# A gated mix of linear attention and experts: two subtractions of the weight preparation stand behind the last sum of a group's seventh slot instead of in front of it

## The chip, the cores and the metric

The kernel runs on one core of a Trainium2 chip. The metric is the time of one execution in device microseconds (us), from runs on the chip. Beside the runs there is one execution that was recorded by the hardware profiler; its trace is what the sections on the profile read.

TensorE (PE) multiplies matrices, with its weight loads shown apart (PEld). VectorE (DVE) and ScalarE (ACT) work element by element and read PE's results out of PSUM. GpSimd (POOL) and SyncE (SP) issue DMA transfers here.

## The reference

Tokens `x` (2048 x 512) go through two branches that a gate mixes. Cut to what matters:

```python
g = sigmoid((x * gate_w).sum(-1))            # the gate, one number for a token
pq, pk = phi(q), phi(k)                      # linear attention, 32 heads of 16
a = (pq @ (pk^T v) / (pq . sum(pk))) @ wo
for e in range(8):                           # all 8 experts, weighted by a softmax
    out += w[e] * (silu(x @ w1[e]) @ w2[e])  # w1[e] 512 x 1792, w2[e] 1792 x 512
return g * a + (1 - g) * out
```

Nearly all of the arithmetic is that of the experts' two layers.

## The kernel before

**Three products for one.** Operands are split into a high part (ScalarE copies the number, rounded to the matmul's type) and a low part (VectorE subtracts the high part from the number). A product is then three matmuls: high by high, high by low, low by high (`mm3`, lines 57 to 60). So every weight and every activation needs one ScalarE copy and one VectorE subtraction, each over 128 x 512 elements as a rule, before TensorE can use it.

**Seven products for eight.** Both layers use a Strassen-like scheme: of two by two blocks seven products are made. That takes sums and differences of blocks on VectorE.

**Groups, slots and ticks.** The first layer runs through 116 groups (an expert, two of its 14 column blocks, one half of the tokens). A group has seven slots, and the loop counter `u` is seven times the group `g` plus the slot `k`. In each slot TensorE does one product of the first layer, six matmuls of 512 columns. In slot 6, the seventh, it does product 5 into the bank `a`, and VectorE then adds that bank to the tile `s3` (line 692). TensorE goes on with product 0 of the next group in the other buffer of `a`, and in slot 1 it adds product 6 of the old group into the old bank `a`: for that the sum of line 692 must have read the bank. From `u` = 45 on there is also a tick of the second layer in every other slot, and from `u` = 72 on in every slot, again six matmuls (`p<-ho,w` in the rows). The activations `ho` that a tick reads are split three ticks or more ahead (line 768).

**The weights one group ahead.** While group `g` runs, `prep(g + 1, step)` splits the raw weights of the next group, a step in a slot. A group's `o` tiles hold the weights of the first layer: `o_0` is ready for product 0, `o_2` serves products 5 and 1, `o_3` products 3 and 4, `o_1` product 6. For the experts' first half of tokens the same steps also make the second layer's weights (`ws`, in the first groups `w` and `wx`) and SP writes them to DRAM (`w2stash`), from where they are loaded again for the ticks (line 793). The `ws` tiles have two buffers that go around.

**Order.** Nothing is scheduled by a tool: each engine runs its instructions in the order in which the program issues them. In a slot `other()` comes first (the step of `prep`, low parts of `ho`, differences between blocks, high parts of `ho`), then the product, then `mid()` with the tick, and last what reads the product's bank.

Of the kernel before, what the change touches and what calls it, by code (L numbers as in the profile page):

```python
# [37 lines left out]
def f32(ap):  # L38
    return ap.bitcast(F32)
# [100 lines left out]
def weights(m):  # L140
    nc, v, w1p, act_copy = m.nc, m.v, m.w1p, m.act_copy

    m.ORDER = ("P1", "P7", "P2", "P4", "P6", "P5", "P3")
    m.SEQ = {n: [(prod, q) for prod in m.ORDER for q in range(n)] for n in (2, NPAIR)}
    last = m.SEQ[NPAIR].pop(NPAIR - 1)
    m.SEQ[NPAIR].insert(2 * NPAIR - 2, last)
    raw, ops, ws = {}, {}, {}
    m.ops = ops
    m.spare = None


    def raw_tile(name, dt=F32):
        return w1p.tile([P, 2048], dt, name=name, tag="rm", bufs=2)


    def with_second(part):
        return part.e < E and part.h == 0

    def load(g):
        if g >= m.NG:  # L160
            return
        part, q = m.groups[g]
        both = with_second(part)
        if g >= m.G1 + 2:
            r = w1p.tile([P, 2 * D], F32, name=f"rs{g}", tag="ws", bufs=2)
            r = raw[g] = r.rearrange("p (r h w f) -> p r h w f", r=2, h=2, w=1)
        else:
            r = raw[g] = raw_tile(f"rm{g}").rearrange("p (r h w f) -> p r h w f", r=2, h=2, w=2)
        for i in range(2):
            if part.e < E:  # L170
                src = m.wm[part.e * NPAIR + q][:, i]
                nc.sync.dma_start(r[:, i, :, 0, :], src[:, :D].rearrange("p (h f) -> p h f", h=2))
            else:
                src = m.wq.rearrange("p (h k c f) -> p h k c f", h=2, k=2, c=KT)
                for h in range(2):
                    nc.sync.dma_start(r[:, i, h, 0, :].rearrange("p (k f) -> p k f", k=2), src[:, h, :, 2 * q + i, :])
        if both:
            for i in range(2):
                src = m.wm[part.e * NPAIR + q][:, i, D:]
                nc.sync.dma_start(r[:, :, i, 1, :], src.rearrange("p (h f) -> p h f", h=2))  # L180

    def two(o, c):
        return o[:, c].rearrange("p (h f) -> p h f", f=HALF)

    def o_tile(name, tag, bufs, width):
        return w1p.tile([P, 2, width], F32R, name=name, tag=tag, bufs=bufs)

    def stash(part, q, prod, src):
        i = part.e * 7 * NPAIR + m.SEQ[part.n].index((prod, q))
        nc.sync.dma_start(m.w2stash[i // 2][:, i % 2].rearrange("p (c f) -> p c f", c=2), f32(src))  # L190

    def prep(g, step):
        if g >= m.NG:
            return
        part, q = m.groups[g]
        r = raw[g]
        both = with_second(part)

        def high(n, src, *places):
            o = o_tile(f"o{g}_{n}", "o", 4, D)
            act_copy(two(o, 0), src)
            for i, at in places:
                ops[g][i] = o, at

        def low(i, src):
            o = ops[g][i][0]
            v.tensor_sub(two(o, 1), src, f32(two(o, 0)))  # L209


        def ws_tile(n):
            w = ws[g, n] = m.spare(f"wx{g}_{n}") if m.spare and n < 3 else o_tile(f"ws{g}_{n}", "ws", 2, D)
            return w

        def high2(n, src):
            if both:
                act_copy(two(ws_tile(n), 0), src)

        def low2(n, src, *prods):  # L220
            if both:
                w = ws.pop((g, n))
                v.tensor_sub(two(w, 1), src, f32(two(w, 0)))  # L223
                for half, prod in enumerate(prods):
                    stash(part, q, prod, w[:, :, half * HALF:(half + 1) * HALF])


        begin = part is m.parts[0] and q < 6

        def first(c):  # L230
            return m.first_w2(q)[:, c] if begin else ws[g, 0][:, c, :HALF]

        def block(i, j):
            return r[:, i, j] if both else r[:, i, j, 0]

        if step == 0:
            ops[g] = [None] * 7
            high(0, r[:, 0, :, 0], (0, 0), (2, HALF))
        elif step == 1:
            low(0, r[:, 0, :, 0])  # L240
            o = o_tile(f"o{g}_1", "oh", 2, HALF)
            act_copy(o[:, 0], r[:, 1, 1, 0])
            ops[g][6] = o, 0
            if both and not begin:
                ws_tile(0)
            if both:
                act_copy(first(0), r[:, 0, 0, 1])
            high2(1, r[:, :, 1, 1] if both else None)
        elif step == 2:
            o = ops[g][6][0]  # L250
            v.tensor_sub(o[:, 1], r[:, 1, 1, 0], f32(o[:, 0]))
            if both:
                v.tensor_sub(first(1), r[:, 0, 0, 1], f32(first(0)))
                stash(part, q, "P1", m.first_w2(q) if begin else ws.pop((g, 0))[:, :, :HALF])
        elif step == 3:
            low2(1, r[:, :, 1, 1] if both else None, "P2", "P4")
            v.tensor_add(block(1, 1), block(1, 0), block(1, 1))
        elif step == 4:
            v.tensor_sub(block(1, 0), block(0, 0), block(1, 0))
            v.tensor_sub(block(0, 0), block(1, 1), block(0, 0))  # L260
        elif step == 5:
            high(2, r[:, 1, :, 0], (5, 0), (1, HALF))
            high2(2, r[:, :, 0, 1] if both else None)
            v.tensor_sub(block(0, 1), block(0, 1), block(0, 0))
        elif step == 6:
            low(5, r[:, 1, :, 0])
            low2(2, r[:, :, 0, 1] if both else None, "P6", "P7")
            high(3, r[:, 0, :, 0], (3, 0), (4, HALF))
            high2(3, r[:, :, 1, 1] if both else None)
        else:  # L270
            low(3, r[:, 0, :, 0])
            low2(3, r[:, :, 1, 1] if both else None, "P3", "P5")


    wp = {}

    def load_wp(q):
        wp[q] = raw_tile(f"wr{q}")[:, :2 * D].rearrange("p (r h f) -> p r h f", r=2, h=2)
        for i in range(2):
            nc.sync.dma_start(wp[q][:, :, i], m.wpd[2 * q + i].rearrange("p (r f) -> p r f", r=2))  # L280

    def prep_wp(q, step):
        r = wp[q]

        def high(n, src):
            act_copy(two(wp["w"][n % 2], 0), src)

        def low(n, src, *prods):
            w = wp["w"][n % 2]
            v.tensor_sub(two(w, 1), src, f32(two(w, 0)))  # L290
            for half, prod in enumerate(prods):
                stash(m.A[0], q, prod, w[:, :, half * HALF:(half + 1) * HALF])

        if step == 0:
            both = raw_tile(f"ww{q}", F32R).rearrange("p (n c f) -> p n c f", n=2, c=2)
            wp["w"] = [both[:, n] for n in range(2)]
            act_copy(wp["w"][0][:, 0, :HALF], r[:, 0, 0])
            high(1, r[:, :, 1])
        elif step == 1:
            w = wp["w"][0]  # L300
            v.tensor_sub(w[:, 1, :HALF], r[:, 0, 0], f32(w[:, 0, :HALF]))
            stash(m.A[0], q, "P1", w[:, :, :HALF])
        elif step == 2:
            low(1, r[:, :, 1], "P2", "P4")
        elif step == 3:
            v.tensor_add(r[:, 1, 1], r[:, 1, 0], r[:, 1, 1])
            v.tensor_sub(r[:, 1, 0], r[:, 0, 0], r[:, 1, 0])
        elif step == 4:
            v.tensor_sub(r[:, 0, 0], r[:, 1, 1], r[:, 0, 0])
            v.tensor_sub(r[:, 0, 1], r[:, 0, 1], r[:, 0, 0])  # L310
        elif step == 5:
            high(2, r[:, :, 0])
            high(3, r[:, :, 1])
        elif step == 6:
            low(2, r[:, :, 0], "P6", "P7")
        else:
            low(3, r[:, :, 1], "P3", "P5")

    m.raw_tile, m.load, m.prep, m.load_wp, m.prep_wp = raw_tile, load, prep, load_wp, prep_wp

def keys(m):
# [208 lines left out]
    beside = {t: [] for t in range(NTT, NT)}  # L532
    for k in range(KT):
# [4 lines left out]
        beside[(10, 10, 12, 12)[k]].append(lambda k=k: x_sum(1, k))  # L538
        beside[(11, 11, 13, 13)[k]].append(lambda k=k: x_part(1, (1, 5, 3, 6)[k]))
        beside[14].append(lambda k=k: m.prep(0, k))  # L540
        beside[15].append(lambda k=k: m.prep(0, 4 + k))
    rows_of = {12: (12, 13), 13: (14, 15), 14: (), 15: ()}
    for t in range(NTT, NT):
        if t in (4, 8):
# [27 lines left out]
def experts(m, misc):  # L572
# [541 lines left out]
    for u in range(LAG + NTICK):  # L1114
# [3 lines left out]
        g, k = divmod(u, 7)  # L1118
# [43 lines left out]
        if u < NU + 3:  # L1162
            up(g, k, mid, other)
        else:
            other()
            mid()
        if u == 5:
            state()
        if u == 6:
# [79 lines left out]
```

## Time and profile before

| | |
|---|---|
| median of 3 runs | 2334.76 us (2334.21 to 2335.16) |
| the profiled execution, its own time | 2334.37 us |
| its span, first to last instruction | 2332.7 us |
| TensorE busy | 2324.6 us, 100% of the span |
| weight loads (PEld) | 1926.1 us, 83% |
| VectorE busy | 1802.6 us, 77% |
| ScalarE busy | 1404.4 us, 60% |
| GpSimd busy | 162.3 us, 7% |

The profiled execution's own time is 1.7 us more than its span, for what lies before the first and behind the last instruction. Busy shares are means over stages that differ: VectorE is over 80% busy up to some 1100 us, while second-layer weights are prepared, and about 72% later. TensorE's matmuls overlap, each is shown with some 390 ns while one starts about every 226 ns; so a busy share of 100% tells that it hardly idles, and the time lost shows in the distance from one matmul's start to the next.

### The profile page before, as it was taken

The page shows a single profiled execution, that of the slowest core. Times are in us where ns is not written, and L with a number is a line of the kernel's source. Part 1 is how long each engine was busy: PE and PEld are TensorE (multiplying, and loading weights), DVE is VectorE, ACT ScalarE, POOL GpSimd, SP SyncE. Part 2 cuts the span into 40 slices and gives each one's busy share as a digit, 9 for nine tenths or more (in the row PEclk, how much of TensorE's full clock was granted, in tenths as well). Part 3 has the DMA queues.
Part 4 walks back from the last instruction along what each step waited for, and adds up shares of the span by engine and source line. Part 5 has one row for each costly group of instructions (what it writes and reads, how often), then busy time and mean ns, then how long its engine had stood idle before and what let it go on. Part 6 is the DMA issues. An engine that isn't in the chain of part 4 may idle for free.

```text
span 2332.7 us, 31250 instructions
## 1 busy us (share of the span) xinstructions
PE 2324.6 (100%) x10444; PEld 1926.1 (83%) x10444; DVE 1802.6 (77%) x3100; ACT 1404.4 (60%) x2631; POOL 162.3 (7%) x223
## 2 busy tenths in 40 slices
PE   9999999999999999999999999999999999999999
PEld 8878888888888888888888888888888888888887
DVE  6798878888888878888666777777677677776676
ACT  6687666666666657666555555555565555555553
POOL 1101000000000000000000000000011010000011
PEclk9999999999999999999999999999999999999999
DMA  7898888988888898888846566566557756565576
GB/s 228 232 306 260 279 276 257 280 261 266 267 268 276 257 286 259 265 267 270 292 145 191 164 208 180 159 190 184 158 166 191 219 163 200 172 190 171 151 241 206
DMA packets 313425, 524.92 MB, mean 225 GB/s; under 512 B 26976, under 2 KB 205296, under 8 KB 312880
## 3 DMA queue, kind: packets, MB, share of 16 engines
q1 hardware_dynamic: 286848, 471.85, 61.6%
q0 software_dynamic: 25568, 50.43, 11.4%
q8 instruction: 82, 1.34, 0.2%
q14 instruction: 79, 0.65, 0.1%
q10 hardware_dynamic: 848, 0.66, 0.1%
HBM read 351.04 MB, written 167.59 MB: 222 GB/s over the span
## 4 chain that ended last, share of the span: by engine, by line
PE 97%; DVE 1%; DMA 1%; ACT 0%; issue 0%; SPq 0%; POOL 0%; DVEq 0%; POOLq 0%
PE p L58 16%; PE p L60 16%; PE p L59 16%; PE a L58 9%; PE a L60 9%; PE a L59 9%; PE c L60 4%; PE c L58 4%; PE c L59 4%; PE b L60 2%; PE b L58 2%; PE b L59 2%; PE g L445 2%; PE y L58 1%; PE y L60 1%; PE y L59 1%
## 5 line engine op out<-in xcount | busy, mean ns | idle before, releaser
L58 PE MATMUL p<-ho,w 128*128 128x512 f32 x1620 | 631.4, 390 | 0.9 <-DVE d L859 0.6
L60 PE MATMUL p<-ho,w 128*128 128x512 f32 x1620 | 630.4, 389 | 0.0
L59 PE MATMUL p<-ho,w 128*128 128x512 f32 x1620 | 630.3, 389 | 0.0
L768 DVE TENSOR_TENSOR ho<-s,ho 128x512 fp32r<-128x512 f32 x784 | 537.0, 686 | 71.0 <-ACT ho L63 67.3
L63 ACT ACTIVATE ho<-s 128x512 fp32r<-128x512 f32 x784 | 487.1, 623 | 22.0 <-PE p L60 10.4
L58 PEld LDWEIGHTS p<-ho,w 128*128 128x128 f32 x1620 | 304.1, 188 | 66.8 <-ACT p L63 2.3
L60 PEld LDWEIGHTS p<-ho,w 128*128 128x128 f32 x1620 | 304.0, 188 | 63.3
L59 PEld LDWEIGHTS p<-ho,w 128*128 128x128 f32 x1620 | 304.2, 188 | 62.8
L686 DVE TENSOR_TENSOR s<-c,s 128x512 f32<-128x512 f32 x116 | 80.2, 691 | 205.2 <-PE c L60 190.2
L63 ACT ACTIVATE o<-rs 128x512 fp32r<-128x512 f32 x224 | 129.2, 577 | 175.9 <-PE a L60 117.6
L63 ACT ACTIVATE o<-rm 128x512 fp32r<-128x512 f32 x240 | 137.5, 573 | 99.5 <-PE a L60 77.7
L63 ACT ACTIVATE ws<-rm 128x512 fp32r<-128x512 f32 x203 | 114.8, 573 | 76.7 <-DMA w2stash<-ws 69.6
L63 ACT ACTIVATE s<-a 128x512 f32<-128x512 f32 x116 | 69.4, 598 | 146.9 <-PE a L60 146.9
L615 ACT ACTIVATE s<-s 128x512 f32<-128x512 f32 x224 | 138.8, 620 | 14.5 <-DVE s L692 10.8
L615 ACT ACTIVATE s<-b 128x512 f32<-128x512 f32 x112 | 67.1, 599 | 107.0 <-PE b L60 106.9
L209 DVE TENSOR_TENSOR o<-rm,o 128x512 fp32r<-128x512 f32 x180 | 123.0, 683 | 0.7 <-ACT o L63 0.6
L209 DVE TENSOR_TENSOR o<-rs,o 128x512 fp32r<-128x512 f32 x168 | 114.7, 683 | 0.6 <-ACT o L63 0.6
L692 DVE TENSOR_TENSOR s<-a,s 128x512 f32<-128x512 f32 x116 | 79.9, 689 | 36.5 <-PE a L60 36.5
L223 DVE TENSOR_TENSOR ws<-rm,ws 128x512 fp32r<-128x512 f32 x154 | 105.5, 685 | 2.2 <-ACT ws L63 2.2
L63 ACT ACTIVATE b<-a 128x512 f32<-128x512 f32 x116 | 67.2, 579 | 56.8 <-PE a L60 56.7
L830 POOL DMA_DIRECT2D acct<-c x30 | 26.1, 871 | 880.7 <-DVE c L824 866.5
L63 ACT ACTIVATE s<-c 128x512 f32<-128x512 f32 x116 | 69.0, 595 | 27.2 <-PE c L60 27.1
(304 smaller groups left out, 4491.3 us busy)
## 6 DMA issues: line engine op xcount, KB each, us to landing
w<-w2stash SPq DMA_DIRECT2D x403, 512.0 KB, 4.1
w2stash<-ws SPq DMA_DIRECT2D x357, 256.0 KB, 4.4
rm<-wm SPq DMA_DIRECT2D x228, 256.0 KB, 5.1
rs<-wm SPq DMA_DIRECT2D x108, 256.0 KB, 4.1
wb<-wgtd SPq DMA_DIRECT2D x16, 512.0 KB, 5.8
acct<-c POOLq DMA_DIRECT2D x30, 256.0 KB, 6.1
acct<-d POOLq DMA_DIRECT2D x30, 256.0 KB, 5.8
acct<-k POOLq DMA_DIRECT2D x30, 256.0 KB, 5.8
```

The lines of the kernel that those rows point to most:

```text
L58: nc.tensor.matmul(ps, wh, xh, start=start, stop=False, skip_group_check=True)
L59: nc.tensor.matmul(ps, wh, xl, start=False, stop=False, skip_group_check=True)
L60: nc.tensor.matmul(ps, wlo, xh, start=False, stop=stop, skip_group_check=True)
L63: nc.scalar.activation(dst, src, AF.Copy, scale=scale, bias=bias)
L209: v.tensor_sub(two(o, 1), src, f32(two(o, 0)))
L223: v.tensor_sub(two(w, 1), src, f32(two(w, 0)))
L445: nc.tensor.matmul(ps, xk((0, 0, 1)[j], tb, k, tt * P, (tt + 1) * P), gw[g][:, (0, 1, 0)[j], k, :], start=(k == 0 and j == 0), stop=(k == ...
L615: nc.scalar.activation(dst, src, AF.Silu)
L686: v.tensor_add(sn[g, 2], bank[g, "c"], sn[g, 2])
L692: v.tensor_add(sn[g, 3], bank[g, "a"], sn[g, 3])
L768: v.tensor_sub(h[1], s, f32(h[0]))
L830: nc.gpsimd.dma_start(m.acct[part.h, j, dt], s, accum_op=ALU.add)
```

## The change

Step 6 of `prep` made the low part of `o_2` and, where there are second-layer weights, that of `ws_2`, and then two high parts. The two low parts are now a step of their own, 8, which is called in slot 6 after the product, the tick and the sum of line 692. The two high parts stay in step 6. Ahead of the main loop, where steps 4 to 7 of group 0 are called one after the other, the order is now 4, 5, 6, 8, 7.

```diff
-        elif step == 6:
+        elif step == 8:
             low(5, r[:, 1, :, 0])
             low2(2, r[:, :, 0, 1] if both else None, "P6", "P7")
+        elif step == 6:
             high(3, r[:, 0, :, 0], (3, 0), (4, HALF))
             high2(3, r[:, :, 1, 1] if both else None)
...
-        beside[15].append(lambda k=k: m.prep(0, 4 + k))
+        beside[15].append(lambda k=k: m.prep(0, (4, 5, 6, 8)[k]))
+    beside[15].append(lambda: m.prep(0, 7))
...
         else:
             other()
             mid()
+        if k == 6:
+            prep(g + 1, 8)
         if u == 5:
             state()
```

What this does to the order: TensorE, ScalarE, GpSimd and SP have the same instructions in the same order as before. VectorE has the same instructions, and from group 0's slot 6 on two of them (one where there are no second-layer weights) move down in each group. Two places of VectorE's order follow. Line numbers of the changed kernel are two higher from the main loop's functions on.

The first place is group 0's slot 6, where a one-off step of the attention branch, `kvt` (line 906, 908 after), comes behind the slot. `s_0<-c` is the sum of slot 5, `s_0<-a` that of slot 6. Before:

```order
L264 TENSOR_TENSOR rm_1206<-rm_1206 128x256
L686 TENSOR_TENSOR s_0_1426<-c_1395,s_0_1426 128x512
L209 TENSOR_TENSOR o_2_1428<-rm_1206,o_2_1428 128x512
L692 TENSOR_TENSOR s_0_1402<-a_1379,s_0_1402 128x512
L906 TENSOR_TENSOR kvt<-kv,mask 128x512
L209 TENSOR_TENSOR o_3_1456<-rm_1206,o_3_1456 128x512
```

And after:

```order
L264 TENSOR_TENSOR rm_1206<-rm_1206 128x256
L688 TENSOR_TENSOR s_0_1426<-c_1395,s_0_1426 128x512
L694 TENSOR_TENSOR s_0_1402<-a_1379,s_0_1402 128x512
L209 TENSOR_TENSOR o_2_1428<-rm_1206,o_2_1428 128x512
L908 TENSOR_TENSOR kvt<-kv,mask 128x512
L209 TENSOR_TENSOR o_3_1455<-rm_1206,o_3_1455 128x512
```

The low part of `o_2` has gone from ahead of the sum to between the sum and `kvt`; group 1 has no second-layer weights, so it is one instruction.

The second place is group 5's slot 6, the first with a low part of `ho` (line 768, 770 after) in it. Before:

```order
L686 TENSOR_TENSOR s_5_1987<-c_1956,s_5_1987 128x512
L209 TENSOR_TENSOR o_2_1989<-rm_1820,o_2_1989 128x512
L223 TENSOR_TENSOR wx_2_1991<-rm_1820,wx_2_1991 128x512
L768 TENSOR_TENSOR ho_1979<-s_2_1677,ho_1979 128x512
L692 TENSOR_TENSOR s_5_1963<-a_1926,s_5_1963 128x512
L209 TENSOR_TENSOR o_3_2005<-rm_1820,o_3_2005 128x512
L223 TENSOR_TENSOR ws_3_2007<-rm_1820,ws_3_2007 128x512
```

And after:

```order
L688 TENSOR_TENSOR s_5_1987<-c_1956,s_5_1987 128x512
L770 TENSOR_TENSOR ho_1979<-s_2_1677,ho_1979 128x512
L694 TENSOR_TENSOR s_5_1963<-a_1926,s_5_1963 128x512
L209 TENSOR_TENSOR o_2_1989<-rm_1820,o_2_1989 128x512
L223 TENSOR_TENSOR wx_2_1991<-rm_1820,wx_2_1991 128x512
L209 TENSOR_TENSOR o_3_2001<-rm_1820,o_3_2001 128x512
L223 TENSOR_TENSOR ws_3_2003<-rm_1820,ws_3_2003 128x512
```

The two low parts have moved down by two places; the low part of `ho` and the sum each stand two places further up. In later groups a difference between blocks can stand beside the `ho`, and it moves up with it.

## Rows read from the trace of the kernel before

**Rows 1.** The page's span, and the busy time of each engine, its share of the span and its instructions.

```profile
span 2332.7 us, 31250 instructions
PE 2324.6 (100%) x10444; PEld 1926.1 (83%) x10444; DVE 1802.6 (77%) x3100; ACT 1404.4 (60%) x2631; POOL 162.3 (7%) x223
```

**Rows 2.** Busy time by stretch of 100 us: the stretch and its length, then busy us and instructions of PE, PEld, DVE, ACT and POOL, the granted clock of TensorE as a share of full speed, the DMA share and GB/s.

```profile
100.00:200.00 100.00, 98.72 (x441) 78.92 (x440) 81.81 (x139) 75.36 (x146) 4.53 (x9) 1.00 0.90 288
...
400.00:500.00 100.00, 100.00 (x443) 82.81 (x442) 84.43 (x141) 63.33 (x119) 5.14 (x6) 1.00 0.88 272
```

**Rows 3.** Who waited for whom over the whole span: the engine, the tile and line that waited, what ended it, us in total, times, the longest.

```profile
DVE s L692 <- PE a L60: 36.5, 79, 3.6
...
PEld a L58 <- DVE s L692: 4.0, 6, 1.1
```

**Rows 4.** The timeline of TensorE at the six places that the last row counts: start, length, line, tiles. In each pair the first row is the last matmul of product 0 (`a<-x00h`), the second row the second matmul of product 6 (`a<-t6l`); one matmul (`a<-t6h`, L58) starts between them.

```profile
123.94 0.39 PE L60 MATMUL a<-x00h,o 128*128 128x512 f32 x1
...
124.61 0.40 PE L59 MATMUL a<-t6l,o 128*128 128x512 f32 x1
...
134.06 0.39 PE L60 MATMUL a<-x00h,o 128*128 128x512 f32 x1
...
135.48 0.39 PE L59 MATMUL a<-t6l,o 128*128 128x512 f32 x1
...
144.57 0.39 PE L60 MATMUL a<-x00h,o 128*128 128x512 f32 x1
...
145.24 0.40 PE L59 MATMUL a<-t6l,o 128*128 128x512 f32 x1
...
154.37 0.39 PE L60 MATMUL a<-x00h,o 128*128 128x512 f32 x1
...
155.03 0.40 PE L59 MATMUL a<-t6l,o 128*128 128x512 f32 x1
...
164.16 0.39 PE L60 MATMUL a<-x00h,o 128*128 128x512 f32 x1
...
165.43 0.40 PE L59 MATMUL a<-t6l,o 128*128 128x512 f32 x1
...
221.00 0.39 PE L60 MATMUL a<-x00h,o 128*128 128x512 f32 x1
...
222.16 0.39 PE L59 MATMUL a<-t6l,o 128*128 128x512 f32 x1
```

**Rows 5.** The timeline of VectorE in slots 5 and 6 of group 3, with idle time and what ended it in brackets, and last the end of product 5 on TensorE.

```profile
142.35 0.69 DVE L686 TENSOR_TENSOR s<-c,s 128x512 f32<-128x512 f32 x1 [0.63 <-PE c L60]
142.96 0.68 DVE L209 TENSOR_TENSOR o<-rm,o 128x512 fp32r<-128x512 f32 x1
143.56 0.69 DVE L223 TENSOR_TENSOR wx<-rm,wx 128x512 fp32r<-128x512 f32 x1
144.16 0.68 DVE L692 TENSOR_TENSOR s<-a,s 128x512 f32<-128x512 f32 x1
...
143.21 0.39 PE L60 MATMUL a<-t5h,o 128*128 128x512 f32 x1
```

**Rows 6.** The timeline at group 0's slot 6, VectorE, the weight load and TensorE: `wp<-wo,kvt` is a matmul that reads `kvt`.

```profile
108.76 0.69 DVE L692 TENSOR_TENSOR s<-a,s 128x512 f32<-128x512 f32 x1 [3.59 <-PE a L60]
...
109.37 0.68 DVE L906 TENSOR_TENSOR kvt<-kv,mask 128x512 f32<-128x512 f32 x1
...
110.10 0.30 PEld L910 LDWEIGHTS wp<-wo,kvt 128*128 128x128 f32 x2 [0.45 <-DVE kvt L906]
```

**Rows 7.** The timeline in group 2, around the step from slot 5 to slot 6: ScalarE copies bank `a`, which slot 4 left (`s<-a`), and TensorE goes from product 4 (`c<-x11h`) to product 5 into that bank (`a<-t5h`, then `a<-t5l`).

```profile
130.78 0.59 ACT L63 ACTIVATE s<-a 128x512 f32<-128x512 f32 x1
...
131.01 0.39 PE L60 MATMUL c<-x11h,o 128*128 128x512 f32 x1
...
131.76 0.39 PE L59 MATMUL a<-t5l,o 128*128 128x512 f32 x1
```

**Rows 8.** The timeline in group 9, slots 5 and 6, and group 10, slots 1 to 3: VectorE's two sums, ScalarE's copy of weights that waits for a DMA to DRAM, its copy into the second layer's bank (`p<-p`), and TensorE around the tick that uses this bank.

```profile
217.42 0.69 DVE L686 TENSOR_TENSOR s<-c,s 128x512 f32<-128x512 f32 x1 [0.25 <-PE c L60]
...
221.08 0.68 DVE L692 TENSOR_TENSOR s<-a,s 128x512 f32<-128x512 f32 x1
...
226.64 0.63 ACT L63 ACTIVATE ws<-rm 128x512 fp32r<-128x512 f32 x1 [1.47 <-DMA w2stash<-ws]
...
228.31 0.58 ACT L63 ACTIVATE p<-p 128x512 f32<-128x512 f32 x1
...
228.54 0.39 PE L60 MATMUL b<-x01h,o 128*128 128x512 f32 x1
...
229.28 0.39 PE L59 MATMUL p<-ho,w 128*128 128x512 f32 x1
```

**Rows 9.** A later stretch: VectorE's read of a second-layer bank in slot 0 of a group; then a load of second-layer weights that SP issues behind the writes of a slot 0, how long a load takes from issue to landing there, and the first matmul of the tick that reads it.

```profile
717.53 0.69 DVE L824 TENSOR_TENSOR e<-p,wb 128x512 f32<-128x512 f32 x1 [1.59 <-PE p L60]
...
358.05 0.41 SPq L793 DMA_DIRECT2D w<-w2stash  x1
...
DMA to landing us min/median/max: 6.9/6.9/6.9
...
367.81 0.39 PE L58 MATMUL p<-ho,w 128*128 128x512 f32 x1
```

## The prediction

> **What bounds the kernel now.** I read the page first: TensorE is busy for 2324.6 of 2332.7 us [rows 1], so only what lets TensorE start a matmul sooner or later can move the end. The view by stretches tells where it loses anything: from 300 to 2200 us every 100 us hold 443 matmuls (one such stretch is shown), which is one each 100/443 = 0.226 us and is the pace of an unbroken row; between 100 and 200 us there are 441, with TensorE busy for 98.72 us [rows 2]. The clock is granted in full in both. So in the long middle there is nothing to win, only to lose.
>
> The waits then tell what the sum of line 692 has to do with it. In 79 of 116 groups VectorE sits idle in front of it, waiting for TensorE, 36.5 us in total; in 6 groups it is the other way round and TensorE's weight load waits for the sum [rows 3]. TensorE's timeline shows these six places, all before 230 us [rows 4]. From the last matmul of product 0 to the second matmul of product 6 an unbroken row takes 2 x 0.226 = 0.45 us. It took 0.67, 1.42, 0.67, 0.66, 1.27 and 1.16 us, so the losses are 0.22, 0.97, 0.22, 0.21, 0.82 and 0.71: 3.15 us together. That is the most that an earlier sum can give.
>
> **The change, first part: the sum comes sooner.** Where VectorE arrives late, two subtractions in front of the sum go away. Their starts and the sum's lie 0.60 us apart (142.96, 143.56, 144.16 [rows 5]), so the sum can start up to 1.20 us sooner, but not before product 5 has ended. In group 3 that is at 143.21 + 0.39 = 143.60, so the sum starts at some 143.65 in place of 144.16 and ends near 144.35, while product 6 could start at 144.57 + 0.23 = 144.80. The wait of 0.22 goes. Groups 1 and 4 have the same pattern and size. Group 2 lost 0.97 and has 1.20 to gain; group 5 lost 0.82. In group 5 a low part of `ho` stays in front of the sum, but its high part was made a slot earlier, so it holds nothing up. In group 9 `ho` and a difference stay in front: from 217.42 three places of 0.60 put the sum at 219.2 in place of 221.08 [rows 8]. All six waits should go.
>
> **Second part: what takes some of it back.** Two places downstream are held by ScalarE, not by VectorE.
> In group 2 product 5 waits for ScalarE's copy that ends at 130.78 + 0.59 = 131.37; the row from 131.01 to 131.76 is 0.30 longer than 0.45 [rows 7]. ScalarE works without a pause from 120 us to there and nothing in it depends on the sum being early, so the 0.22 won in group 1 is waited off here. Left: 3.15 - 0.22 = 2.93.
> In group 10 a tick waits for `p<-p`, with 228.54 to 229.28 again 0.29 longer than 0.45; ScalarE is late because it waited 1.47 us for the write of a `ws` tile to DRAM [rows 8]. This write belongs to `ws_3`, whose low part is the third subtraction behind the new place of the sum: some 219.2 + 4 x 0.60 = 221.6 against 222.3 now (the sum at 221.08, two places on). If the write lands as much sooner, ScalarE moves by 0.65 while TensorE has moved by 0.71, a loss of 0.06. If it does not, because the write of `ws_2` now goes out right in front of it, the whole 0.71 is waited off. Bounds 0.06 and 0.71; I take 0.06, since VectorE's row decides when the write can start.
>
> **Third part: what is now behind the sum.** The subtractions wait with it. In group 0 the sum had to wait 3.59 us for TensorE, so the subtraction moved out of that idle time to behind the sum, in front of `kvt`. And `kvt` is waited for: the weight load of `wp<-wo,kvt` starts at 110.10, right behind the end of `kvt` at 109.37 + 0.68 = 110.05 [rows 6]. One place of 0.60 us later for `kvt` is 0.60 later for TensorE, and nothing later in group 1 was waiting for something else long enough to swallow it. Cost 0.60.
>
> In all other groups the tail behind the sum starts up to 1.20 us later than now. What must be ready: `o_2` for product 1. In the groups without ticks 12 matmuls (products 0 and 6) lie between the end of product 5 and product 1, 2.7 us, and the third matmul there, the first to read the low part, starts 0.45 us later still. `o_2` is done at about 0.05 + 0.60 + 0.69 = 1.34 us. Slack 1.8 us. With ticks there are 30 matmuls between. `o_3` is needed two slots later. The reads of the second layer's banks come next: in the group shown VectorE waits 1.59 us for TensorE in front of such a read [rows 9], more than 1.20, so the read is not delayed.
>
> SP issues the same transfers in the same order, but the writes of `ws_2` and `ws_3` are ready later, and it holds the loads behind them. The tightest load that I found goes out at 358.05 and lands 6.9 us later, at 364.9; its tick starts at 367.81 [rows 9], so 2.9 us are to spare and 1.20 is used. Cost nothing; with the cover gone, see the second rival.
>
> **A rule beside it.** Rows 5 show a VectorE that does nothing in front of a sum for which it is waiting although subtractions lie ready behind it. The Trainium skill, PSUM — Partial Sum Buffer, section Engine vs sequencer instructions, says that VectorE's queue is strictly first in, first out, so by it every subtraction that is put behind a waiting sum inherits the wait. In group 0 the trace would show that as the 0.60 above. It speaks against this change in 79 of 116 groups; by this rule alone, with each inherited wait passed on to TensorE, the kernel would lose some 79 x 0.60 = 47 us. The slacks above are why I do not follow it so far; it has 0.01 of the 0.08 that the slower cases get below.
>
> **The sum.** -3.15 + 0.22 + 0.06 + 0.60 = -2.27. From the profiled execution's own 2334.37 us that is 2332.1. The median of the runs lies 0.39 above the profiled one, so I predict 2332.5 us, 0.10% less. I take 0.2%, 4.7 us, as what a measurement of this kernel can tell from no change; so the forecast is no change.
>
> **Rivals.**
> *All gaps close and nothing comes back.* By the Trainium skill, Perfetto Trace Analysis, section Optimization Strategy, one finds the gaps of the busiest engine and makes what they wait for start sooner. Worked out from rows: the full 3.15, and if group 0's `kvt` were hidden too, 2331.6. Against it: ScalarE's copy at 130.78 and the row at 110.10. Still no change by 0.2%. Chance 0.10. To pass 0.2% this way more than all six gaps would have to go; for that I leave 0.03 beside it, for waits that the trace does not show.
> *SP becomes the bound, slower.* Loads like that of 358.05 come about once in two groups, 38 us, between 230 and 1110 us: some 23. If the writes in front of them come 1.20 later by VectorE, and the transfers, now closer together, take longer too, a load is late once the shift is over 2.9 us. Each 0.3 us beyond costs 23 x 0.3 = 7 us: at a shift of 3.5 us 23 x 0.6 = 14 us, less the 2.3, gives 2346. For it: SP is in order, and DMA is 0.88 busy there [rows 2]. Against it: 1.7 us of slack left. Chance 0.08.
> *The gain is waited off at the next place.* If the write for group 10 does not land sooner (0.71), and group 2's or 5's wait only moves to ScalarE or to a low part of `ho`, 0.7 to 1.7 more comes back: 2333.2 to 2334.8, and with a new wait of a few tenths in some of the eight groups that hand over a bank in slot 1, 2336. Chance 0.22.
>
> **How the numbers follow.** Forecast as worked out, 2331.7 to 2333.2: 0.57. All gaps, 0.10; waited off, 0.22; slower, 0.08; faster by over 0.2%, 0.03. The range from 2331.5 to 2335.2 takes in the first two and most of the third, about 0.85. Faster 0.03, within 0.2% 0.89, slower 0.08.
>
> **What would show it.** Right: weight loads of `a` no longer wait for the sum, or once; TensorE's pairs at product 0 and product 6 all at 0.45; the wait for `kvt` up from 0.45 to about 1.05; VectorE's idle time in front of the sum up by some 79 x 1.2 = 95 us, with less idle time behind it; 443 matmuls in every stretch from 300 to 2200 us. Wrong: fewer than 443 in any of these stretches, waits of `p` for a load `w`, or the six gaps still there under another name (ScalarE, `ho`).

## The result, and the profile after

The changed kernel takes 2347.31 us (median of 4 runs, 2345.53 to 2348.77), the kernel before in the same comparison 2334.95 us (4 runs, 2334.21 to 2335.16): ratio 1.0052, 95% interval 1.004 to 1.0065. It is slower by 12.4 us, where 2332.5 was predicted, with 2335.2 as the upper end of the range. The profiled execution took 2345.53 us. It is the fastest of the four; the others took 1.5 to 3.2 us longer, at a mean granted clock of 0.999 in place of 1.00, and the account below is for the profiled one alone.

First the page of the changed kernel, in the columns of [rows 1]: the span has grown by 11.1 us, TensorE's busy time by only 3.0, so that it stands more.

```profile
span 2343.8 us, 31203 instructions
PE 2327.6 (99%) x10444; PEld 1926.7 (82%) x10444; DVE 1802.4 (77%) x3100; ACT 1398.8 (60%) x2631; POOL 161.7 (7%) x223
```

The stretches, in the columns of [rows 2], show where: of the 443 matmuls that nearly every 100 us held from 300 us on, 438, 433 and 432 are left in the stretches below, at a full clock.

```profile
300.00:400.00 100.00, 99.49 (x438) 81.72 (x437) 81.63 (x137) 63.31 (x121) 1.80 (x2) 1.00 0.84 270
400.00:500.00 100.00, 99.18 (x438) 81.83 (x437) 83.19 (x138) 61.97 (x119) 5.14 (x6) 1.00 0.86 272
...
700.00:800.00 100.00, 97.96 (x433) 80.78 (x432) 81.56 (x138) 62.17 (x119) 5.17 (x6) 1.00 0.83 258
...
1000.00:1100.00 100.00, 97.85 (x432) 80.72 (x431) 83.40 (x140) 63.71 (x122) 3.45 (x4) 1.00 0.81 259
```

The waits of the changed kernel, in the columns of [rows 3] (L694 is line 692 of before, L770 is 768):

```profile
ACT ws L63 <- DMA w2stash<-ws: 169.2, 100, 4.9
DVE ho L770 <- ACT ho L63: 136.0, 103, 4.5
DVE s L694 <- PE a L60: 79.9, 82, 4.2
PEld p L58 <- ACT p L63: 13.0, 14, 2.6
PEld p L58 <- DMA w<-w2stash: 2.0, 5, 0.6
PEld c L58 <- ACT s L63: 1.5, 1, 1.5
```

The same waits before, as far as they are among the long ones there:

```profile
DVE ho L768 <- ACT ho L63: 70.0, 68, 2.9
ACT ws L63 <- DMA w2stash<-ws: 69.6, 67, 2.2
...
PEld p L58 <- ACT p L63: 2.3, 5, 0.6
```

The weight loads of `a` no longer wait for the sum, as foreseen. But TensorE now waits 13.0 us for ScalarE's copies into second-layer banks (`p`), and ScalarE has waited 100 us longer for writes of `ws` tiles to DRAM.

**The account, matmul by matmul.** Both traces have the same 10444 matmuls in the same order on TensorE, so the start of each can be set against that of the same one before. The table gives how much this difference grows over each place. Between the places it drifts by some hundredths, which are counted with the place behind.

| place (time in the trace before) | change of the difference, us |
|---|---|
| first 100 us, ahead of any moved instruction | +0.82 |
| `wp<-wo,kvt`, 110 us | +0.60 |
| six places of [rows 4] | -3.28 |
| group 2's product 5, 131 us | +0.25 |
| group 8's product 4, into bank `c`, 200.6 us | +1.32 |
| a tick of group 10, 227 us | +0.16 |
| hand-over of a bank in group 10, 228.9 us | +1.07 |
| eight later hand-overs, 362 to 1029 us | +8.69 |
| loads of `w`, at 597, 825, 1146, 1155 us | +1.10 |
| everything else | +0.05 |
| sum | +10.78 |

The first row is not the change's: in the traces of the experiments the same stretch differs by -0.23 to +1.33. The change itself costs 13.2 us and gives 3.3 back. The hand-overs carry 9.76 of the 13.2. They are the places where in slot 1 a second-layer bank passes from one product to the next: ScalarE copies the old bank (`k<-p`), then fills in the start value of the new one (`p<-p`; in three of the nine, at 381, 648 and 915 us, the kept copy, `p<-k`), and only then TensorE can begin the tick that uses the bank, in slot 3.

The 1.32 at 200.6 us have the same look in the first layer. ScalarE stands for 4.90 us at a `ws` copy, in place of 2.20 before, its copy out of bank `c` comes behind that, and TensorE waits for it (the last of the waits above):

```profile
198.69 0.63 ACT L63 ACTIVATE ws<-rm 128x512 fp32r<-128x512 f32 x1 [4.90 <-DMA w2stash<-ws]
```

**One hand-over in rows.** Here is the one at 762 us before and 768 us after. Up to there the same matmul starts 4.33 us later in the trace after (766.31 - 761.98, the last one ahead of the tick), so 4.33 is to be taken off its times. First before: VectorE, SP, ScalarE and TensorE, from the sum of slot 5 to the tick.

```profile
748.88 0.69 DVE L686 TENSOR_TENSOR s<-c,s 128x512 f32<-128x512 f32 x1 [0.30 <-PE c L60]
...
750.09 0.69 DVE L223 TENSOR_TENSOR ws<-rm,ws 128x512 fp32r<-128x512 f32 x1
...
750.80 0.87 SPq L190 DMA_DIRECT2D w2stash<-ws  x2
752.88 0.33 SPq L793 DMA_DIRECT2D w<-w2stash  x1
753.81 0.87 SPq L190 DMA_DIRECT2D w2stash<-ws  x2
...
758.54 0.63 ACT L63 ACTIVATE ws<-rm 128x512 fp32r<-128x512 f32 x1 [0.61 <-DMA w2stash<-ws]
...
760.21 0.58 ACT L63 ACTIVATE p<-p 128x512 f32<-128x512 f32 x1
...
761.98 0.39 PE L60 MATMUL b<-x01h,o 128*128 128x512 f32 x1
762.21 0.39 PE L58 MATMUL p<-ho,w 128*128 128x512 f32 x1
```

And after:

```profile
754.73 0.68 DVE L688 TENSOR_TENSOR s<-c,s 128x512 f32<-128x512 f32 x1
...
756.53 0.69 DVE L694 TENSOR_TENSOR s<-a,s 128x512 f32<-128x512 f32 x1
757.13 0.68 DVE L209 TENSOR_TENSOR o<-rm,o 128x512 fp32r<-128x512 f32 x1
757.73 0.69 DVE L223 TENSOR_TENSOR ws<-rm,ws 128x512 fp32r<-128x512 f32 x1
...
758.94 0.69 DVE L223 TENSOR_TENSOR ws<-rm,ws 128x512 fp32r<-128x512 f32 x1
...
758.48 0.87 SPq L190 DMA_DIRECT2D w2stash<-ws  x2
759.45 0.45 SPq L795 DMA_DIRECT2D w<-w2stash  x1
759.98 0.95 SPq L190 DMA_DIRECT2D w2stash<-ws  x2
...
766.44 0.63 ACT L63 ACTIVATE ws<-rm 128x512 fp32r<-128x512 f32 x1 [4.06 <-DMA w2stash<-ws]
...
768.11 0.58 ACT L63 ACTIVATE p<-p 128x512 f32<-128x512 f32 x1
...
766.31 0.39 PE L60 MATMUL b<-x01h,o 128*128 128x512 f32 x1
768.74 0.50 PE L58 MATMUL p<-ho,w 128*128 128x512 f32 x1 [2.04 <-ACT p L63]
```

The chain that ended last runs through here; this is its step from the issue of the second half of `ws_3`'s write to its landing (start, length):

```profile
760.44 5.90 DMA w2stash<-ws
```

Step by step, on before's time: the low part of `ws_2` starts at 757.73 - 4.33 = 753.40 in place of 750.09, 3.31 later. Of these, 1.52 are there already at the sum of slot 5 (754.73 - 4.33 = 750.40 in place of 748.88), and 1.79 are the three instructions that it has been moved past. SP's writes of `ws_2` go out 3.35 later (754.15), the load of `w` behind them 2.24 later, the write of `ws_3` 1.84 later (755.65). The three transfers, which before went out over 3.0 us, now leave within 1.5, and the last half takes 5.90 us to land. ScalarE's copy of the next group's `ws_1`, which needs the buffer that `ws_3` had, starts at 762.11 in place of 758.54, 3.57 later; `p<-p` likewise. The tick had 762.21 - (760.21 + 0.58) = 1.42 to spare, so 2.15 are left over. TensorE's first matmul came 2.20 later here, and the second lost another 0.11.

So the working theory for the experiments was: **theory 1**, the time is lost where ScalarE's hand-over copy stands in its queue behind a `ws` copy that waits for the write of `ws_3`, and that write is late because `ws_2` and `ws_3` are. The rival, **theory 2**: the moved work itself, or late loads on SP, cost the time, and the copies are a symptom.

### The profile page after: what moved, and what is told of

Read it like the earlier page. It is cut to its first block, busy times and chain, and to the rows that moved or that the text cites. A ratio compares the mean times of both kernels' runs of the same rounds, so it can differ in the third digit from the quotient of the medians.

```text
span 2343.8 us, 31203 instructions
## 1 busy us (share of the span) xinstructions
PE 2327.6 (99%) x10444; PEld 1926.7 (82%) x10444; DVE 1802.4 (77%) x3100; ACT 1398.8 (60%) x2631; POOL 161.7 (7%) x223
## 4 chain that ended last, share of the span: by engine, by line
PE 91%; DVE 3%; DMA 3%; ACT 1%; issue 1%; SPq 0%; POOL 0%; ACTq 0%; DVEq 0%; POOLq 0%
PE p L58 15%; PE p L60 14%; PE p L59 14%; PE a L58 8%; PE a L60 8%; PE a L59 8%; PE c L60 4%; PE c L59 4%; PE c L58 4%; DMA w2stash<-ws 2%; PE g L446 2%; PE b L60 2%; PE b L58 2%; PE b L59 2%; DVE ho L770 1%
## 5 line engine op out<-in xcount | busy, mean ns | idle before, releaser
L770 DVE TENSOR_TENSOR ho<-s,ho 128x512 fp32r<-128x512 f32 x784 | 537.0, 686 | 137.1 <-ACT ho L63 133.5
L58 PE MATMUL p<-ho,w 128*128 128x512 f32 x1620 | 632.8, 391 | 8.4 <-ACT p L63 7.2
L58 PEld LDWEIGHTS p<-ho,w 128*128 128x128 f32 x1620 | 304.1, 188 | 78.9 <-ACT p L63 13.0
L694 DVE TENSOR_TENSOR s<-a,s 128x512 f32<-128x512 f32 x116 | 80.0, 690 | 80.5 <-PE a L60 79.9
```

Source lines behind the costliest of these rows:

```text
L58: nc.tensor.matmul(ps, wh, xh, start=start, stop=False, skip_group_check=True)
L694: v.tensor_add(sn[g, 3], bank[g, "a"], sn[g, 3])
L770: v.tensor_sub(h[1], s, f32(h[0]))
```

## The experiments

Their times are compared with runs of the kernel before on the same chip, whose medians were 2335.43, 2335.28 and 2335.06 us.

**One low part at a time.** In the first run only the low part of `o_2` stands behind the sum, in the second only that of `ws_2`.

```diff
         elif step == 8:
             low(5, r[:, 1, :, 0])
-            low2(2, r[:, :, 0, 1] if both else None, "P6", "P7")
         elif step == 6:
+            low2(2, r[:, :, 0, 1] if both else None, "P6", "P7")
```

> Of the two subtractions only the low part of o_2 stands behind the sum; that of ws_2 stays in front. Theory 1 (the write of ws_2, and right behind it that of ws_3, reaches DRAM too late, ScalarE's copy into the next group's ws_1 waits for it, and the hand-over of a second-layer bank stands behind this copy): the write of ws_2 is as early as before and that of ws_3 only 0.6 us later, so most of the loss goes: 2333 to 2337 us, ScalarE's waits for w2stash 70 to 110 us against 169 after the change. Theory 2 (VectorE's longer tail behind the sum makes what TensorE reads late, whichever subtraction it is): about half of the loss stays, 2339 to 2343 us. Theory 3 (SP issues the loads of second-layer weights late): the same as theory 1 in time, but TensorE's waits are for w, not for p.

> Only the low part of ws_2 stands behind the sum; that of o_2 stays in front. Theory 1: the write of ws_2 moves as far as in the full change and stands next to that of ws_3, which is 0.6 us later: a good part of the loss stays, 2339 to 2346 us, and TensorE waits for p behind ScalarE. Theory 2: half of the loss, 2339 to 2343 us, as much as with o_2 alone. The pair tells: theory 1 wants this one slower than the one with o_2 alone by at least 4 us, theory 2 wants them equal.

Measured: 2335.54 us (ratio 0.9999, 0.999 to 1.0008) with `o_2` alone, 2341.22 us (1.0025, 1.0016 to 1.0034) with `ws_2` alone. ScalarE's wait for the writes, first with `o_2` alone, then with `ws_2` alone:

```profile
ACT ws L63 <- DMA w2stash<-ws: 77.3, 73, 2.7
```

```profile
ACT ws L63 <- DMA w2stash<-ws: 155.6, 91, 5.0
```

The low part that feeds a DMA costs the time. The one that only TensorE reads costs nothing on balance, and next to nothing behind 230 us: in its trace the six places give back 1.7, and 0.60 at `kvt`, 0.24 at 131 us and 0.62 at group 10's hand-over go again. The two don't add up: 0.1 and 5.8 alone, 12.4 together, and at the nine hand-overs alone 0.6 and 6.5 against 9.8. Where the sum waits for TensorE, `o_2` in front of it fills this wait, while `o_2` behind it makes `ws_2` up to a place of 0.60 us later still. With the hand-overs already past their slack, each such place costs again.

**Where it pays and where it costs.** The low parts stand behind the sum only in loop groups 1 to 5 and 9, those whose sum TensorE waited for; in the other run, in all groups but these.

```diff
+    EARLY = (2, 3, 4, 5, 6, 10)     # g of prep(g, ...), one more than the loop's group
...
+        if step == 6 and g > 0 and g not in EARLY:
+            prep(g, 80)
+        elif step == 8 and g > 0 and g not in EARLY:
+            return
...
-        elif step == 8:
+        elif step in (8, 80):
```

> The two subtractions stand behind the sum only in the slots of groups 1 to 5 and 9, where TensorE waited for the sum; in all others, group 0 with kvt too, they stand in front. Theory 1: the gains of the six places without the later cost: 3.15 less 0.2 to 0.9 that ScalarE waits off at groups 2 and 10, 2332.0 to 2333.5 us, and 443 matmuls in every 100 us after 300. If the loss comes from the early groups instead: 2340 us or more.

> The complement: the two subtractions stand behind the sum in all groups but 1 to 5 and 9. Theory 1: the loss of the change without its gains: 12.4 + 2 to 3, 2346 to 2351 us, with the six waits for the sum back and TensorE's waits for p at the hand-over of the second-layer banks. If the loss comes from the early groups: 2335 us.

Measured: 2332.17 us (0.9986, 0.9977 to 0.9995) early, 2354.37 us (1.0077, 1.0064 to 1.009) late. In the early run's trace the six places give back 3.25 us, group 2 takes 0.24 of it and group 10's hand-over 0.53, and there is no further step of more than 0.13 up to the end. The later stretches hold what they held before:

```profile
700.00:800.00 100.00, 100.00 (x443) 82.84 (x442) 82.14 (x139) 65.00 (x123) 4.31 (x5) 1.00 0.89 273
1000.00:1100.00 100.00, 100.00 (x443) 82.81 (x442) 85.31 (x143) 64.32 (x123) 4.31 (x5) 1.00 0.84 261
```

The complement came out slower than expected. Its trace puts 9.9 us on the hand-overs from 362 us on (8.7 in the changed kernel), 1.6 on slow matmuls behind one of them (last section), 1.6 on the place at 200.6 us and 1.2 on late loads of `w`; and the six early waits are back, group 9's longer by 1.32 than before.

**Taking the hand-over out from behind the wait.** ScalarE's copy of `ws_1` is issued at the end of slot 1, behind the tick and the hand-over, in place of at its beginning; everything else as in the changed kernel. The same edit was made on the kernel before.

```diff
             if both:
                 act_copy(first(0), r[:, 0, 0, 1])
+        elif step == 9:
             high2(1, r[:, :, 1, 1] if both else None)
...
+        if k == 1:
+            prep(g + 1, 9)
```

> The changed kernel, with one more edit: ScalarE's high copy of ws_1, which stands in slot 1 in front of everything else that ScalarE does in that slot, is issued behind the slot's tick and the hand-over copies of the second layer's bank. Theory 1 (the hand-over copies are late because they stand in ScalarE's queue behind a ws copy that waits for the write of ws_3): the nine waits of TensorE for the copies p, some 9.8 us, go; the early gain of 3.15 less kvt's 0.60 and group 2's 0.28 stays, and a new wait may arise because ws_1 is late for its own low part and its write: 2332 to 2338 us, with ScalarE's wait for the write of a ws tile still there (fewer than 169 us, since the copy asks later). Theory 2 (the moved work itself, or transfers that come late to TensorE, cost the time): the copies p are not what matters and the time stays at 2345 to 2349.

> The kernel before, with the same edit of ws_1's high copy alone. It shows what this edit is worth where the two low parts stand in front of the sum. Theory 1: before lost 0.29 us to a hand-over copy, so nothing is to be had beyond that: 2334 to 2336 us. Theory 2: the same. If it is faster by more than 2 us, then the edit has a value of its own and the result of the run with both edits has to be reduced by it.

Measured: 2336.98 us (1.0008, 0.9999 to 1.0017), and on the kernel before 2335.34 us (1.0, 0.9991 to 1.0009). So the edit has no value of its own, and with it the changed kernel loses 1.7 us against the kernel before, in place of 12.4. ScalarE in its trace, at the hand-over shown above:

```profile
758.60 0.58 ACT L63 ACTIVATE p<-p 128x512 f32<-128x512 f32 x1
...
760.95 0.63 ACT L63 ACTIVATE ws<-rm 128x512 fp32r<-128x512 f32 x1 [1.27 <-DMA w2stash<-ws]
```

And two of its waits:

```profile
ACT ws L63 <- DMA w2stash<-ws: 127.6, 86, 4.0
DVE ho L771 <- ACT ho L63: 68.4, 69, 2.8
```

The wait for the write is still there, but `p<-p` now comes ahead of it, and no hand-over behind 230 us costs TensorE anything. This decides for theory 1: the moved work is the same, and at five of the nine hand-overs the write of `ws_3` goes out as late as in the changed kernel, within 0.2 us (at the other four 0.35 to 1.8 sooner, 0.67 at the one above). VectorE comes back in time too: its sum of slot 5 above starts 0.15 us later than before, in place of 1.52. Against the early run it loses 0.60 at `kvt`, 0.44 at 200.6 us, 0.66 at a sum at 207 us, 0.20 at group 9's sum, 0.68 at a low part of `ho` at 227 us, and 1.2 to late loads of `w`; group 10's hand-over is 0.72 better.

**What holds the write of `ws_3`.** The low part of `ws_3` is put ahead of that of `o_3` in step 7; then, after this run's result, the low part of `ws_2` ahead of that of `o_2` in step 8.

```diff
         else:
-            low(3, r[:, 0, :, 0])
             low2(3, r[:, :, 1, 1] if both else None, "P3", "P5")
+            low(3, r[:, 0, :, 0])
```

> The changed kernel, with the low part of ws_3 in front of that of o_3 in VectorE's order, so that ws_3's write can go out one place (0.60 us) sooner. Theory 1 (ScalarE's copy of ws_1 waits for this write, and at nine hand-overs TensorE waits for what stands behind that copy): each of the waits of more than 0.60 us shrinks by up to 0.60, the smaller ones go, together some 4 to 5 us: 2341 to 2344 us. If the write only queues longer behind that of ws_2, the gain is smaller, 2344 to 2346. Theory 2 (the write of ws_3 is not what holds the hand-over): 2347, or more if o_3 is late.

```diff
         elif step == 8:
-            low(5, r[:, 1, :, 0])
             low2(2, r[:, :, 0, 1] if both else None, "P6", "P7")
+            low(5, r[:, 1, :, 0])
```

> The changed kernel, with the two moved low parts in the other order: the sum, then ws_2, then o_2. ws_2's writes can go out one place (0.60 us) sooner; ws_3's low part stands where it stood. It follows the run with ws_3 ahead of o_3, which did not get ws_3's write out sooner: in that trace SP issued ws_2's two writes and a load first, and these took 1.50 us as in the changed kernel. Theory 1a (SP's three issues behind ws_2's low part set when ws_3's write goes out): ws_3's write goes out up to 0.35 to 0.60 us sooner, until its own low part sets it, and the hand-overs wait less by that: 2341 to 2345 us, near the run in which ws_2 alone was moved (2341.22). Theory 1b (only the order to ScalarE and the sum of moved work count, not ws_2's place): 2346 to 2349 us as the changed kernel.

Measured: 2350.58 us (1.0069, 1.0057 to 1.0082) with `ws_3` first, a miss, and 2338.90 us (1.0015, 1.0006 to 1.0024) with `ws_2` first. SP's issues at the same hand-over, first with `ws_3` first:

```profile
761.95 0.87 SPq L190 DMA_DIRECT2D w2stash<-ws  x2
762.91 0.44 SPq L795 DMA_DIRECT2D w<-w2stash  x1
763.45 0.95 SPq L190 DMA_DIRECT2D w2stash<-ws  x2
```

and with `ws_2` first:

```profile
753.61 0.87 SPq L190 DMA_DIRECT2D w2stash<-ws  x2
754.57 0.45 SPq L795 DMA_DIRECT2D w<-w2stash  x1
755.38 0.91 SPq L190 DMA_DIRECT2D w2stash<-ws  x2
```

From the first write of `ws_2` to the first of `ws_3` SP takes 759.98 - 758.48 = 1.50 us in the changed kernel and 763.45 - 761.95 = 1.50 with `ws_3` first, one issue right behind the other. So it is the end of `ws_2`'s low part, and SP's own pace behind it, that sets `ws_3`'s write; an earlier `ws_3` finds SP busy. With `ws_2` first the distance is 1.77, and `ws_3`'s low part sets it. This run's hand-overs cost 4.3 us in place of 9.8, a gain of more than 0.60 at some of the nine (2.35 to 1.03 at the one above), and the time is 2 us below the expected range.

The likely amplifier is in the waits above; no run changes it alone. While ScalarE stands at the `ws` copy, the high parts of `ho` behind it wait too, then VectorE's low parts of `ho` (70.0 us before, 136.0 after, 68.4 with the hand-over taken out), and VectorE comes late to the next sums. In the rows above `s<-c` starts 1.52 later than before, and without waiting for TensorE. That lateness is handed to the next `ws_2`.

The run with `ws_3` first is worse than the changed kernel by 3.3 us in the medians, and by 7.8 in the two profiled executions (the slowest of its five against the fastest of four); in these its hand-overs cost 1.3 us more, late loads of `w` 2.7 more, and slow matmuls 3.1 (last section). That the loads are late because `o_3` is, which holds the raw weights longer, was not tested.

**Both edits together.** Early groups only, with the copy of `ws_1` behind the hand-over.

> The two low parts behind the sum only in those groups whose sum TensorE waited for (loop groups 1 to 5 and 9), and the high copy of ws_1 behind the slot's tick and hand-over in all groups. The first edit alone gave 2332.17 us. Theory 1: the remaining waits of that kernel are 0.69 us in group 2 and 0.92 us at a hand-over near 226 us, of which the second may go: 2331 to 2332.5 us. Theory 2 (the order of ScalarE's copies does not matter): 2332 to 2332.5.

Measured: 2331.76 us (0.9985, 0.9976 to 0.9994), 3.5 us faster than the kernel before. The loss of 0.53 at group 10's hand-over is gone from the trace; against the early run alone the 0.4 us are too little to be told apart by times. It beats both kernels.

Whether a third buffer for `ws` would take away the wait itself was not tried. How much of the 5.90 us of landing is queueing behind the other transfers, and how much is the write's own, stays open.

## Why the prediction was wrong, step by step

*What bounds the kernel*: right. "In the long middle there is nothing to win, only to lose" is what happened, though not every stretch there holds 443 matmuls: two hold 442, the last two 446 and 453.

*First part, the sum comes sooner, -3.15*: right. All six waits are gone: in the changed kernel, as in the run with the early groups alone, each of the six pairs takes 0.45, together 3.1 less than before. In group 3 the sum starts right behind product 5, as worked out from [rows 5]: 144.11 with 0.41 of waiting for TensorE. For group 9 the mechanism was off: VectorE comes to it late, the sum starts some 0.8 sooner and not 1.9. That was enough, since it ends at 221.35 and product 6 starts at 221.65 in the trace after.

*Second part, given back at ScalarE*: group 2 right (0.22 foreseen, 0.25 measured). Group 10 was taken at 0.06, with 0.71 as its other end, and came to 1.07. The choice between the ends was wrong, and the upper end too low: the low part of `ws_3` was to start 0.65 sooner and started 0.4 later, and the early groups alone cost 0.53 there.

*Third part*: `kvt` right, 0.60 foreseen and 0.60 measured; its weight load now waits 1.05 in place of the 0.45 of [rows 6]:

```profile
111.53 0.30 PEld L912 LDWEIGHTS wp<-wo,kvt 128*128 128x128 f32 x2 [1.05 <-DVE kvt L908]
```

`o_2` right: alone behind the sum it costs next to nothing behind 230 us. **The step that failed is the sentence on all other groups.** It let the tail start "up to 1.20 us later", named as its next readers VectorE's read of a second-layer bank and SP's loads, and put their cost at nothing. Measured are 8.7 us at eight hand-overs and 1.3 at 200.6 us. Three things were missed. A moved subtraction is later not by the two places that the sum gains but by all that it is moved past, here `ho`, a difference and the sum, 1.79; and where VectorE is already late, or the sum stands waiting for TensorE, that comes on top. So `ws_2` came 3.31 later in the rows above and not 1.20. SP issues its write in order with the others, so the write of `ws_3` inherits it. And that write has a reader that the text itself had shown in [rows 8], ScalarE's copy into the ring's next buffer; it was priced in group 10 and then not looked for in the eight other groups that hand over a bank in slot 1. There it stood at 0.61 of waiting with 1.42 of slack behind it, in the rows of before above.

*The rivals*: the third, "waited off at the next place", named the place (groups that hand over a bank in slot 1) and priced it at "a few tenths"; measured were 0.3 to 2.45 each, in nine places, 9.8 together. The second, SP as the bound, had the right size (2346) by a wrong path: late loads cost 1.1 of the 13.2. Its ground, that transfers closer together take longer, fits the row of 5.90, which is shown for a write and not a load.

*The rule beside it*: the Trainium skill, PSUM — Partial Sum Buffer, section Engine vs sequencer instructions, states strict first in, first out for ScalarE's queue as well as for VectorE's. For VectorE the trace agrees (idle in front of the sum 36.5 before [rows 3], 79.9 after), and the 47 us worked out from it did not come, because most of that idle time is covered. Some is not. At the hand-over of 496 us VectorE is in time at the sum of slot 5, and `ws_2` is still 2.65 later: 1.8 for what it is moved past, and the rest is the wait of the sum, which it inherits:

```profile
487.17 0.69 DVE L694 TENSOR_TENSOR s<-a,s 128x512 f32<-128x512 f32 x1 [0.76 <-PE a L60]
```

For ScalarE I did not apply the rule; the rows of `ws<-rm` (4.06) and `p<-p` behind it are that case.

*What would show it*: fewer than 443 matmuls in a stretch and waits for a load `w` were named as the signs of a wrong forecast; both are there. VectorE's idle time in front of the sum was to grow by some 95 us and grew by 43: at places such as the one at 762 us VectorE comes too late to wait (756.53 above).

## What to carry to other kernels

When an instruction is moved down, follow what it feeds: count its delay by everything that it passes, and where it feeds a DMA, go on to the transfers issued behind that one, to the ring buffer that the last of them frees, and to whatever stands in line behind the one who waits for that buffer. A slack has to be read at each kind of place where the chain ends on the bound engine, the rare ones too: here 9 hand-overs out of hundreds of ticks, with one copy of the first layer that stood in the same line, carried 11.1 of the 13.2 us lost. And a change that pays in six groups and costs in others should be made in the six.

## What was not expected of the hardware

After two pauses of TensorE at hand-overs the clock fell. In the run with `ws_3` first the rows behind a pause, and the stretch's clock (columns of [rows 2]), read (first TensorE's timeline, then the stretch):

```profile
1044.71 0.51 PE L58 MATMUL p<-ho,w 128*128 128x512 f32 x1 [1.86 <-ACT p L63]
1045.06 0.59 PE L59 MATMUL p<-ho,w 128*128 128x512 f32 x1
1045.45 0.63 PE L60 MATMUL p<-ho,w 128*128 128x512 f32 x1
1045.87 0.63 PE L58 MATMUL p<-ho,w 128*128 128x512 f32 x1
```

```profile
1040.00:1050.00 10.00, 8.14 (x29) 6.22 (x28) 6.24 (x10) 5.88 (x12) 0.00 (x0) 0.83 0.97 310
```

For eight matmuls the distance is 0.43 us in place of 0.226, the lower of the clock's two levels, 1.2 of 2.4 GHz. Here TensorE had stood 2.25 us from one start to the next, at the other place 2.75; the two cost 3.1 us beside the pauses. In the changed kernel's profiled execution pauses of 2.43 and 2.54 us left the clock at 1.00. In the run that leaves out the six early groups, one of 2.79 was followed by eight slow matmuls and one of 2.27 was not. So a pause of this length can cost twice, and one trace does not tell whether it will.

At the hand-over shown, the same transfers took longer when they were issued closer together. The two writes of `ws_3` (256 KB each) were waited for until 758.54 - 753.81 = 4.73 us behind their first issue before, and until 766.44 - 759.98 = 6.46 us after. Ahead of them went 1 MB in both cases, two writes and a load, over 753.81 - 750.80 = 3.01 us before and over 1.50 us after. With `ws_3` first it was 6.51 us at 1.50, with `ws_2` first 6.15 at 1.77. What in the transfers takes the longer time, these traces do not tell.
